# A feed-forward layer with its gradients: Square and Gelu ahead of evictions, a gate product ahead of a cubic, and two tails over 128 rows

## The chip, the core and the metric

The kernel runs on one core of a Trainium2 chip. The core has TensorE (PE, matmuls from SBUF into the eight PSUM banks), VectorE (DVE), ScalarE (ACT), GpSimd (POOL) and SyncE (SP), each with its own in-order queue of instructions; they wait for each other through semaphores. Transfers are issued from the queues of SP, ACT and POOL. The metric is the device time of one execution in microseconds (us), as the median over several runs.

## What is computed

```python
def _fwd_reference(x, w1, b1, w2, b2):        # x (1, 2048, 448), w1 (448, 1792), w2 (1792, 448)
    h = jnp.einsum("bsd,df->bsf", x, w1) + b1
    h = _gelu(h)                              # tanh approximation
    return jnp.einsum("bsf,fd->bsd", h, w2) + b2

def reference(x, w1, b1, w2, b2, grad_out):
    out, vjp = jax.vjp(_fwd_reference, x, w1, b1, w2, b2)
    return (out, *vjp(grad_out))              # out, and gradients of x, w1, b1, w2, b2
```

Everything that comes in and goes out is bfloat16. With u = x w1 + b1 and q = grad_out w2^T, the kernel needs h = gelu(u), gh = gelu'(u) q, out = h w2 + b2, the gradient of x, gh w1^T, and the products over the 2048 rows for the gradients of the weights.

## The kernel before

The 2048 rows are cut into 4 blocks of 512 columns of the transposed data, and the 1792 hidden features into 14 tiles of 128, taken two at a time. A *pair* is one block with two such tiles; there are 28, numbered f or k from 0, seven to a block. For a pair, TensorE computes u into two PSUM banks ("pu") and q into two ("pq"). 448 = 3 x 128 + 64, so each product over the 448 has three full steps (`w1_f`, `w2T`) and a *tail* of 64 rows (`wt1` and the last slice of `xT`). The tails, like most other matmuls, run as 64-row halves of the array, one half beside the other (`half_product`, L259). The pairs 0, 1 and 2 at the start have their full steps over 128 rows (`pe_u_fulls`, L238), and the tails of 0 and 1 run alone, each as two 64-row matmuls (`pe_tails`, which calls `u_tail`).

Around a pair's products stands its elementwise work. ACT copies u with its bias to SBUF (`copy_u`, L339), computes Square (`act_square`, L348), Gelu (`act_gelu`, L345, which gives h), and later the tanh (`act_tanh`, L357). DVE computes the *cubic* from the Square (L376), *cubic\*u* (L378, what the tanh needs), *slope* and *slope\*h* (L380, L382), *both* (L385), *gate* (L387) and *gh*, the gate product, which reads q from PSUM and writes gh (L393). The list of names that `dve_chain` is given is the order of DVE's queue.

The pairs 0 to 11 are worked in *single steps*, i = 1 to 11 in a loop (and pair 0 ahead of it). In step i TensorE does u of pair f = i + 2 and q of pair i. From pair 12 on come *double steps*, n = 0 to 7, with pairs k = 12 + 2n and k + 1 together: `act_tanh`, `dve_gate` (L361 to L368 on both pairs), then gh of k + 1 and of k (`dve_gh`, L393), while TensorE does u of the next two pairs (`pe_u_rows`, in the first double step alone), tails, q (`pe_q_rows`), and u of the pairs after those. Step i = 11 and n = 0 are the *passage*.

A *unit* is 128 rows of out (kind "o", from h) or of the gradient of x (kind "x", from gh), over 28 half-row matmul slots for each of two row halves. When a unit is finished it stands in the list `finished`, and `evictions()` empties its bank: kind "x" on ACT (L431), kind "o" on DVE with the bias (L433), both into one of five staging tiles, from which POOL issues the transfer to the output (L434). In steps 7 to 11 TensorE fills its gaps with four units of kind "x", two in PSUM banks 2 and 3 (`later`) and two in one tile of two banks (`ahead`). Their matmuls stand in the list `slots`, ten slots to a step: 8 of ahead, 14 of later, 7 of ahead, 14 of later, 7 of ahead. The two of `later` finish at slot 43 and the two of `ahead` at slot 50, both in step 11.

The banks turn over. Pair 14's u goes into banks 0 and 1, which `copy_u(13)` frees, pair 15's into banks 2 and 3, which the evictions of `later` free. The q of pair 13 goes into bank pair 1, which the evictions of `ahead` free, and q of pair 12 into bank pair 0, which gh of pair 11 frees. The next units go into bank pair 1 after gh of pair 13.

The weights arrive in pieces by transfers whose order is written out by hand; SP issues most. At i = 6 `other_halves` loads the upper 64 rows of `wt1`, which serve the later blocks; until then only its lower 64 rows (`DL` = 64) hold anything. Block 0's transposed x is loaded 512 wide (`wide`), so its last slice has 64 rows of the tail and 64 rows that belong to the next row of x.

Of the kernel before, what the change touches and what calls it, by code (L numbers as in the profile page):

```python
# [19 lines left out]
def kernel(  # L20
# [15 lines left out]
    nc = tc.nc  # L36
    P = 128
    B, S, D = x.shape
    F = w1.shape[1]
    assert (B, S, D, F) == (1, 2048, 448, 1792)  # L40
    NS = S // P
    NF = F // P
    KF = D // P
    DL = D - KF * P
# [3 lines left out]
    NPAIR = NF // 2  # L48
    NSTEP = NB * NPAIR
    NSINGLE = 12  # L50
# [30 lines left out]
    wt1 = const.tile([P, F], BF16, name="wt1")  # L81
# [12 lines left out]
    xT, gT = {}, {}  # L94
# [44 lines left out]
    AZ = tmp.tile([P, 12, SB], BF16, name="AZ", tag="AZ", bufs=1)  # L139
    zero = AZ[:, 0, :]  # L140
    nc.vector.memset(zero, 0.0)
    nc.gpsimd.memset(b1_rows[:], 0.0)
    nc.gpsimd.dma_start(out=b1_rows[0:NF, :], in_=b1.rearrange("(ft p) -> ft p", p=P))
    xT[0] = blk.tile([P, KF + 1, SB], BF16, name="xT", tag="xT")
# [45 lines left out]
    PU, PQ = {}, {}  # L190
# [4 lines left out]
    def cols(p, a):  # L195
        return slice((2 * FP[p] + a) * P, (2 * FP[p] + a + 1) * P)

    def part_u(ks):
        return U4[:, 2 * (ks[0] % 2):2 * (ks[-1] % 2) + 2, :]
# [4 lines left out]
    def part_a(ks):  # L204
        k = ks[0]
        return place(4 * (k % 3) if k < NSINGLE else SETS[k // 2 % 2] + 2 * (k % 2), ks)

    def part_z(ks):
        k = ks[0]
        return place(4 * (k % 3) + 2 if k < NSINGLE else 4 + 2 * (k % 2), ks)  # L210
# [14 lines left out]
    def open_u(f):  # L225
        b, p = divmod(f, NPAIR)
        if p == 0:
            hT[b] = blk.tile([P, NF, SB], BF16, name="hT", tag="hT")
        banks = (2, 3) if f == 1 else (0, 1) if f < NSINGLE + LEAD else order_a[2 * (f % 2):2 * (f % 2) + 2]
        PU[f] = [one_bank(n, "pu") for n in banks]  # L230

    def pe_u_fulls(f):
        b, p = divmod(f, NPAIR)
        open_u(f)
        for rs in halves if f == 0 else [slice(0, SB)]:
            for a in range(2):
                for kt in range(KF):
                    nc.tensor.matmul(PU[f][a][:, rs], lhsT=w1_f[:, kt, cols(p, a)], rhs=xT[b][:, kt, rs],  # L238
                                     start=(kt == 0 and rs.start == 0), stop=False, skip_group_check=True)
# [4 lines left out]
    def open_q(k):  # L244
        b, p = divmod(k, NPAIR)
        if p == 0:
            ghT[b] = blk.tile([P, NF, SB], BF16, name="ghT", tag="ghT")
        PQ[k] = two_banks(0 if k < NSINGLE else order_b[k % 2], "pq")
# [14 lines left out]
    def u_tail(f, a):  # L263
        b, p = divmod(f, NPAIR)
        hf = half(b not in WIDE)
        half_product(("u", f, a), PU[f][a][:], wt1[hf, cols(p, a)], xT[b][hf, KF, :], hf, False, True)

    def q_tail(k, a, swap=False):
        b, p = divmod(k, NPAIR)
        hf = half((b in WIDE) != swap)  # L270
        g = g_swap[b] if swap else gT[b][:, 0, :]
        half_product(("q", k, a), PQ[k][:, a, :], w2T[hf, 0, cols(p, a)], g[hf, :], hf, True, False)
# [5 lines left out]
    def pe_tails(fs, ks):  # L278
        cross = bool(fs) and bool(ks) and (fs[0] // NPAIR in WIDE) != (ks[0] // NPAIR in WIDE)
        for k in ks:  # L280
            open_q(k)
        us = [(f, a) for f in fs for a in range(2)]
        qs = [(k, a) for k in ks for a in range(2)]
        if not us and len(ks) == 2:
            for a in range(2):
                q_tail(ks[0], a)
                q_tail(ks[1], a, swap=True)
            return
        for n in range(max(len(us), len(qs))):
            if n < len(us):  # L290
                u_tail(*us[n])
            if n < len(qs):
                q_tail(*qs[n], swap=cross)
# [76 lines left out]
    def dve_chain(*names):  # L370
        for name in names:
            op, k = name.split()
            k = int(k)
            a_, z_ = part_a([k]), part_z([k])
            if op == "cubic":
                nc.vector.tensor_scalar(out=z_, in0=a_, scalar1=3.0 * GELU_C, scalar2=None, op0=ALU.add)  # L376
            elif op == "cubic*u":
                nc.vector.tensor_tensor(out=z_, in0=z_, in1=part_u([k]), op=ALU.mult)  # L378
            elif op == "slope":
                nc.vector.tensor_scalar(out=a_, in0=a_, scalar1=GELU_C, scalar2=-2.0, op0=ALU.add, op1=ALU.mult)  # L380
            elif op == "slope*h":
                nc.vector.tensor_tensor(out=a_, in0=a_, in1=rows(hT, [k]), op=ALU.mult)  # L382
            elif op == "both":
                both = place(4 * (k % 3), [k, k])
                nc.vector.tensor_scalar(out=both, in0=both, scalar1=1.0, scalar2=math.sqrt(0.5), op0=ALU.add, op1=ALU.mult)  # L385
            elif op == "gate":
                nc.vector.tensor_tensor(out=z_, in0=z_, in1=a_, op=ALU.mult)  # L387
            else:
                dve_gh(k)
# [20 lines left out]
    class Unit:  # L410
# [13 lines left out]
            self.done += 1  # L424
            self.slots += 4

        def evict(self):
            st = stg.tile([P, SB], BF16, name="st", tag="st")
            r = ROW0[self.b] + self.j * P
            if self.kind == "x":  # L430
                nc.scalar.copy(out=st[:, 0:D], in_=self.ps)  # L431
            else:
                nc.vector.tensor_tensor(out=st[:, 0:D], in0=self.ps, in1=b2_bc[:], op=ALU.add)  # L433
            nc.gpsimd.dma_start(out=(out2 if self.kind == "o" else gx2)[r:r + P, :], in_=st[:, 0:D])  # L434
# [27 lines left out]
                open_units.remove(un)  # L462
                finished.append(un)

    def evictions(most=NS):
        for un in finished[:most]:
            un.evict()
        del finished[:most]

    turns = {6: [(0, 0, 2)], 7: [(0, 2, 4)], 8: [(0, 4, 7)], 9: [(1, 0, 3)], 10: [(1, 3, 5)], 11: [(1, 5, 7)], 12: [(2, 0, 2)],  # L470
# [10 lines left out]
    def traffic(i):  # L481
# [5 lines left out]
        if i == 6:  # L487
            other_halves()

    pe_u_fulls(0)  # L490
    pe_tails([0], [])
    copy_u(0, "av")
    act_square([0])
    act_gelu([0])
    dve_chain("cubic 0", "cubic*u 0")
    pe_u_fulls(1)
    pe_tails([1], [])
    copy_u(1, "av")
    act_tanh([0])
    act_square([1])  # L500
# [23 lines left out]
    def tiles(p):  # L524
        return range(2 * p, 2 * p + 2)
# [13 lines left out]
    for i in range(1, NSINGLE):  # L539
        f = i + LEAD  # L540
        if i < 6:
            between = [(uns[1], False, tiles(i)), (uns[0], True, tiles(i)[:1]), (uns[0], True, tiles(i)[1:]), (uns[1], True, tiles(i))]
        elif i == 6:
            between = [(uns[0], True, tiles(i)), (uns[1], False, tiles(i)[:1]), (uns[1], False, tiles(i)[1:]), (uns[1], True, tiles(i))]
        else:
            if i == 7:
                ahead, later = xs, two_units((2, 3))
                slots = [(ahead, False, t) for t in range(6, NF)] + [(later, False, t) for t in range(NF)]
                slots += [(ahead, True, t) for t in range(NPAIR)] + [(later, True, t) for t in range(NF)]
                slots += [(ahead, True, t) for t in range(NPAIR, NF)]  # L550
            between = [slots[2 * c:2 * c + 2] for c in range(5)]
            del slots[0:10]
        open_u(f)
        open_q(i)
        side_by_side(u_of(f, 0, True), u_of(f, 1, True))
        fill(between[0])
        side_by_side(u_of(f, 1), u_of(f, 0))
        fill(between[1])
        pe_tail_pair(f, i, 1)
        pe_tail_pair(f, i, 0)  # L560
        fill(between[2])
        side_by_side(q_of(i, 0), q_of(i, 1))
        fill(between[3])
        side_by_side(q_of(i, 1, True), q_of(i, 0, True))
        if i < 6:
            units_side(uns[0], False, tiles(i + 1))
        elif i > 6:
            fill(between[4])
        if i > 1:
            act_tanh([i])  # L570
        if i == 6:
            evictions(2)
        copy_u(f, "aa")
        if i > 6:
            evictions()
        act_square([f])
        act_gelu([f])
        if i == 1:
            dve_chain("both 1", "cubic 2", "gate 1", "cubic*u 2", "slope 2", "gh 1", "slope*h 2", "cubic 3")
        elif i < NSINGLE - 1:  # L580
            dve_chain(f"both {i}", f"cubic*u {i + 1}", f"gate {i}", f"slope {i + 1}", f"gh {i}", f"slope*h {i + 1}", f"cubic {f}")
        else:
            dve_chain(f"both {i}", f"cubic*u {i + 1}", f"gate {i}", f"cubic {f}", f"gh {i}", f"cubic*u {f}")
        if i == 6:
            evictions()
            open_two(1, 2)
            xs = open_units[-2:]
            units_side(xs, False, range(0, 6))
        if i == 9:
            nc.gpsimd.dma_start(out=g_low[0:DL, :], in_=gT[1][DL:P, 0, :])  # L590
            g_swap[1] = g_low
        if i < 8 or i % 2:
            traffic(i if i < 8 else (i + 7) // 2)
        if i >= 6:
            stores(1 if i > 7 and i % 2 else 2, f - 1)
# [20 lines left out]
    for n in range(nq):  # L616
        i = 10 + n
# [206 lines left out]
```

## Time and profile before

| | |
|---|---|
| median of 3 runs | 270.81 us (270.75 to 271.07) |
| the profiled execution | 270.53 us |
| its span in the profile | 268.8 us |
| TensorE busy | 261.8 us, 97% of the span |
| VectorE busy | 175.0 us, 65% |
| ScalarE busy | 137.3 us, 51% |
| GpSimd busy | 42.0 us, 16% |
| granted TensorE clock | 0.998 of full speed |

The profile is one execution of the program. Its span runs from the first to the last instruction that it shows, and the execution's own time is 1.73 us longer. A row of a timeline gives the start and the length in us, engine, line of the program, operation, output and input tiles with their shapes, how many such instructions are merged (x2), and in brackets how long the engine stood idle ahead of it and what it waited for. Lengths of successive instructions of one engine overlap a little, since the next one starts in the pipeline before the last has left it; the ends of matmuls are modelled. A busy TensorE is therefore not TensorE at its peak.

### The profile page before, as it was taken

To read this page: it belongs to the slowest core of one execution; us is meant where nothing else is said; L and a number is where in the kernel's file an instruction comes from. 1 tells how busy PE (TensorE), PEld (TensorE's weight loads), DVE (VectorE), ACT (ScalarE), POOL (GpSimd) and SP (SyncE) were. 2 spreads that over 40 slices of the span, in tenths; PEclk is the share of its full clock that TensorE was granted. 3 is DMA by queue.
4 is the path that set the end of the run, shared out by engine and by line. 5 is a ranking of instruction groups with operands and counts; after the bars stand their busy time and mean duration, and the time that the engine had idled before them with its cause. 6 is when DMAs were issued, how large, how long until landed. Compare 5 with 4: busy or idle time off the path is not lost.

```text
span 268.8 us, 5196 instructions
## 1 busy us (share of the span) xinstructions
PE 261.8 (97%) x2170; PEld 164.7 (61%) x2170; DVE 175.0 (65%) x214; ACT 137.3 (51%) x163; POOL 42.0 (16%) x52
## 2 busy tenths in 40 slices
PE   7999999999979999999999999999999999999995
PEld 3356668888636665555657888874444665555554
DVE  1699999998698879687898831219999991000000
ACT  2899998878786867968668410022111111121111
POOL 1002004200302020110202030311600008900000
PEclk9999999999999999999999999999999999999999
DMA  7999999999999956172561449999511102999841
GB/s 176 235 269 198 154 233 193 268 243 217 221 224 232 235 166 156 37 191 50 152 152 41 80 91 272 353 191 238 143 39 39 49 22 48 215 220 214 206 123 34
DMA packets 111735, 44.47 MB, mean 165 GB/s; under 512 B 91040, under 2 KB 110576, under 8 KB 111712
## 3 DMA queue, kind: packets, MB, share of 16 engines
q1 hardware_dynamic: 104608, 36.14, 63.3%
q0 software_dynamic: 1856, 4.30, 5.9%
q10 hardware_dynamic: 5248, 3.71, 4.7%
q8 instruction: 17, 0.28, 0.4%
q14 instruction: 6, 0.05, 0.1%
HBM read 7.23 MB, written 14.23 MB: 80 GB/s over the span
## 4 chain that ended last, share of the span: by engine, by line
PE 94%; DMA 2%; ACT 1%; DVE 1%; issue 1%
PE ps L259 31%; PE ps_v L776 16%; PE pq L259 15%; PE pu L259 14%; PE ps_w L744 14%; PE ps_w L755 2%; DMA xT<-in_x_dram 2%; PE pu L238 2%; DVE ghT L393 1%; ACT U L339 0%; ACT st L431 0%; ACT AZ L348 0%; PE ps L421 0%; DVE AZ L378 0%; ACT st L779 0%
## 5 line engine op out<-in xcount | busy, mean ns | idle before, releaser
L259 PE MATMUL pq<-gT,w2T 64*128 64x512 bf16 x386 | 58.0, 376 | 0.0
L259 PE MATMUL ps<-w_sb,hT 64*128 64x448 bf16 x440 | 52.6, 349 | 1.1 <-DVE ghT L393 1.1
L259 PE MATMUL ps<-w1T_sb,ghT 64*128 64x448 bf16 x448 | 51.2, 349 | 0.0
L259 PE MATMUL pu<-xT,w_f 64*128 64x512 bf16 x300 | 44.0, 376 | 0.8 <-ACT U L339 0.8
L339 ACT ACTIVATE U<-pu,b1T 128x512 bf16<-128x512 f32 x53 | 32.8, 684 | 19.4 <-PE pu L259 19.4
L776 PE MATMUL ps_v<-g_nat,h_nat 128*128 128x448 bf16 (+1 forms) x240 | 42.6, 340 | 0.0
L393 DVE SCALAR_TENSOR_TENSOR ghT<-AZ,pq 128x1024 bf16<-128x1024 bf16 x28 | 33.9, 1219 | 13.3 <-PE pq L259 12.6
L434 POOL DMA_DIRECT2D out_dram<-st x32 | 19.7, 618 | 137.8 <-DVE st L433 75.6
L259 PEld LDWEIGHTS <-ghT 64*128 64x128 bf16 x448 | 33.9, 94 | 10.3
L259 PEld LDWEIGHTS <-hT 64*128 64x128 bf16 x440 | 29.4, 94 | 16.0 <-issue 1.5
L259 PEld LDWEIGHTS <-w2T 64*128 64x128 bf16 x392 | 29.8, 94 | 11.8 <-DMA w2T<-in_w_dram 0.3
L744 PE MATMUL ps_w<-gh_nat,x_nat 128*128 128x512 bf16 (+1 forms) x192 | 36.5, 352 | 0.0
L776 PEld LDWEIGHTS <-h_nat 128*128 128x128 bf16 x240 | 23.3, 98 | 19.3 <-DMA out_dram<-st 0.3
L357 ACT ACTIVATE AZ<-AZ 128x1024 bf16<-128x1024 bf16 (+1 forms) x20 | 27.8, 1390 | 9.0 <-DVE AZ L353 7.3
L730 DVE TENSOR_TENSOR acc<-acc,gh_nat 128x1792 f32<-128x1792 f32 x14 | 30.0, 2142 | 0.5
L744 PEld LDWEIGHTS <-x_nat 128*128 128x128 bf16 x192 | 18.7, 98 | 17.9 <-issue 0.4
L348 ACT ACTIVATE AZ<-U 128x1024 bf16<-128x1024 bf16 (+1 forms) x21 | 28.2, 1341 | 0.9 <-DVE U L341 0.4
L345 ACT ACTIVATE hT<-U 128x1024 bf16<-128x1024 bf16 (+1 forms) x22 | 27.9, 1274 | 0.0
L259 PEld LDWEIGHTS <-w_f 64*128 64x128 bf16 x300 | 21.0, 94 | 11.2 <-issue 1.4
L779 ACT CAST st<-ps_v 128x448 bf16<-128x448 f32 (+1 forms) x15 | 7.6, 507 | 34.8 <-PE ps_v L776 34.8
L431 ACT CAST st<-ps 128x448 bf16<-128x448 f32 x16 | 7.8, 536 | 29.6 <-PE ps L259 28.0
L747 ACT CAST st<-ps_w 128x512 bf16<-128x512 f32 (+1 forms) x12 | 6.4, 532 | 27.8 <-PE ps_w L744 27.8
(52 smaller groups left out, 190.0 us busy)
## 6 DMA issues: line engine op xcount, KB each, us to landing
hT_dram<-hT SPq DMA_DIRECT2D x28, 256.0 KB, 3.5
out_dram<-st POOLq DMA_DIRECT2D x32, 112.0 KB, 4.6
x_nat<-in_x_dram SPq DMA_DIRECT2D x1, 1792.0 KB, 10.3
g_nat<-in_grad_out_dram SPq DMA_DIRECT2D x1, 1792.0 KB, 15.5
out_dram<-st ACTq DMA_DIRECT2D x13, 112.0 KB, 3.3
out_dram<-st ACTq DMA_DIRECT2D x9, 128.0 KB, 1.7
w_f<-in_w_dram SPq DMA_DIRECT2D x5, 192.0 KB, 3.9
w_sb<-in_w_dram SPq DMA_DIRECT2D x4, 224.0 KB, 3.8
```

The costliest lines, as they stand in the source:

```text
L259: mm = nc.tensor.matmul(ps, lhsT=w, rhs=m, start=start, stop=stop, tile_position=(hf.start, 0), skip_group_check=True)
L339: nc.scalar.activation(out=dst, in_=PU[f][a][:], func=ACT.Identity, bias=bias)
L345: nc.scalar.activation(out=rows(hT, r), in_=part_u(r), func=ACT.Gelu_apprx_tanh)
L348: nc.scalar.activation(out=part_a(ks), in_=part_u(ks), func=ACT.Square, scale=math.sqrt(3.0 * GELU_A * GELU_C))
L357: nc.scalar.activation(out=z, in_=z, func=ACT.Tanh, scale=-1.0 / 3.0)
L393: nc.vector.scalar_tensor_tensor(out=rows(ghT, [k]), in0=part_z([k]), scalar=1.0, in1=PQ[k][:], op0=ALU.subtract if single else ALU.add, o ...
L431: nc.scalar.copy(out=st[:, 0:D], in_=self.ps)
L434: nc.gpsimd.dma_start(out=(out2 if self.kind == "o" else gx2)[r:r + P, :], in_=st[:, 0:D])
L730: nc.vector.tensor_tensor(out=v, in0=in0, in1=gh_nat[:, b, :, j, :], op=ALU.add)
L744: nc.tensor.matmul(ps[:, 0:n * P], lhsT=x_nat[:, st_, kt * P:(kt + 1) * P], rhs=gh_nat[:, b, ft0:ft0 + n, j, :], start=(st_ == 0), stop=(s ...
L776: nc.tensor.matmul(ps[:, 0:w], lhsT=h_nat[ft][:, st_, :], rhs=g_nat[:, st_, h * w:(h + 1) * w], start=(st_ == 0), stop=(st_ == NS - 1))
L779: nc.scalar.copy(out=o[:, 0:w], in_=ps[:, 0:w])
```

## The change

Three things are changed.

- At the front, the upper 64 rows of `wt1` in columns 256 to 767 are set to zero by a memset on DVE, and the tails of pairs 0 and 1 run as matmuls over all 128 rows, whose upper half multiplies those zeros.
- In step 11 the evictions are split. ACT evicts the first finished unit ahead of Square 13 and Gelu 13; the second is evicted by DVE with a plain copy, behind gate 11; the last two are left to the call at the start of n = 0, behind Gelu 13. The calls of `evictions()` in steps 7 to 10, ahead of the Square, are gone.
- In the DVE order of step 11, gh 11 stands ahead of cubic 13 instead of behind it.

```diff
     nc.vector.memset(zero, 0.0)
+    nc.vector.memset(wt1[DL:P, 256:768], 0.0)
...
-        def evict(self):
+        def evict(self, by=None):
...
-            if self.kind == "x":
+            if self.kind == "x" and by is not None:
+                nc.vector.tensor_copy(out=st[:, 0:D], in_=self.ps)
+            elif self.kind == "x":
                 nc.scalar.copy(out=st[:, 0:D], in_=self.ps)
...
-    def evictions(most=NS):
+    def evictions(most=NS, by=None):
         for un in finished[:most]:
-            un.evict()
+            un.evict(by)
         del finished[:most]
...
+    def pe_tail_zeros(f):
+        b, p = divmod(f, NPAIR)
+        for a in range(2):
+            nc.tensor.matmul(PU[f][a][:], lhsT=wt1[:, cols(p, a)], rhs=xT[b][:, KF, :], start=False, stop=True, skip_group_check=True)
+
     pe_u_fulls(0)
-    pe_tails([0], [])
+    pe_tail_zeros(0)
...
     pe_u_fulls(1)
-    pe_tails([1], [])
+    pe_tail_zeros(1)
...
         copy_u(f, "aa")
-        if i > 6:
-            evictions()
+        if i == NSINGLE - 1:
+            evictions(1)
         act_square([f])
         act_gelu([f])
...
-            dve_chain(f"both {i}", f"cubic*u {i + 1}", f"gate {i}", f"cubic {f}", f"gh {i}", f"cubic*u {f}")
+            dve_chain(f"both {i}", f"cubic*u {i + 1}", f"gate {i}")
+            evictions(1, "v")
+            dve_chain(f"gh {i}", f"cubic {f}", f"cubic*u {f}")
```

## Prediction

> **What bounds the kernel now.** I read the trace from the outside in. First the busy time by stretch: start, microseconds, then busy time and instruction count of TensorE (PE), weight loads (PEld), VectorE (DVE), ScalarE (ACT) and GpSimd (POOL). The two stretches are the passage from single steps to double steps, and most of what follows it.
>
> ```profile
> 67.67:77.70 10.03, 7.79 (x64) 4.41 (x61) 7.79 (x10) 8.71 (x10) 1.64 (x4) 1.00 1.16 214
> 77.70:222.90 145.20, 145.20 (x1285) 91.02 (x1285) 110.16 (x107) 65.20 (x71) 20.24 (x28) 1.00 0.59 141
> ```
>
> After 77.70 TensorE is busy for all of the 145.20 us, so from there the end moves with the moment at which that stretch begins. In the 10.03 us before it, TensorE works 7.79 us. That is where time can be had, and the next three views, timelines of ACT, DVE and PE through the passage (start, length, instruction, and in brackets the idle time ahead and its releaser), say what the hole hangs on.
>
> ```profile
> 65.16 1.26 ACT L339 ACTIVATE U<-pu,b1T 128x512 bf16<-128x512 f32 x2 [0.67 <-PE pu L259]
> 66.31 0.96 ACT L431 CAST st<-ps 128x448 bf16<-128x448 f32 x2
> 67.68 0.97 ACT L431 CAST st<-ps 128x448 bf16<-128x448 f32 x2 [0.41 <-PE ps L259]
> 68.54 1.07 ACT L348 ACTIVATE AZ<-U 128x1024 bf16<-128x1024 bf16 x1
> 69.49 1.06 ACT L345 ACTIVATE hT<-U 128x1024 bf16<-128x1024 bf16 x1
> 71.83 1.91 ACT L357 ACTIVATE AZ<-AZ 128x2048 bf16<-128x2048 bf16 x1 [1.28 <-DVE AZ L378]
> 73.65 0.67 ACT L339 ACTIVATE U<-pu,b1T 128x512 bf16<-128x512 f32 x1
> ```
>
> ACT copies pair 13's two halves (65.16), evicts two units, waits 0.41 us for TensorE to finish two more units, evicts those (67.68), and only then does Square 13 (68.54) and Gelu 13 (69.49). Inputs of the Square were there at 66.42, where the copies end.
>
> ```profile
> 65.73 0.69 DVE L387 TENSOR_TENSOR AZ<-AZ 128x1024 bf16<-128x1024 bf16 x1
> 69.64 0.43 DVE L376 TENSOR_SCALAR AZ<-AZ 128x1024 bf16<-128x1024 bf16 x1 [3.22 <-ACT AZ L348]
> 69.98 1.21 DVE L393 SCALAR_TENSOR_TENSOR ghT<-AZ,pq 128x1024 bf16<-128x1024 bf16 x1
> 71.11 0.68 DVE L378 TENSOR_TENSOR AZ<-AZ,U 128x1024 bf16<-128x1024 bf16 x1
> 71.71 0.69 DVE L361 TENSOR_SCALAR AZ<-AZ 128x2048 bf16<-128x2048 bf16 x1
> 72.50 1.23 DVE L363 TENSOR_TENSOR AZ<-AZ,hT 128x2048 bf16<-128x2048 bf16 x1
> 73.77 0.69 DVE L364 TENSOR_SCALAR AZ<-AZ 128x2048 bf16<-128x2048 bf16 x1
> 74.37 0.69 DVE L367 TENSOR_SCALAR AZ<-AZ 128x2048 bf16<-128x2048 bf16 x1
> 75.10 1.22 DVE L368 TENSOR_TENSOR AZ<-AZ 128x2048 bf16<-128x2048 bf16 x1
> 76.42 2.35 DVE L393 SCALAR_TENSOR_TENSOR ghT<-AZ,pq 128x1024 bf16<-128x1024 bf16 x2
> ```
>
> DVE stands 3.22 us before "cubic 13" (L376), which needs that Square. Behind it in the same queue stands gate product 11, "gh 11" (L393 at 69.98), which does not need it. From 69.64 to the products 13 and 12 (76.42) DVE has no gap worth naming: it is one chain.
>
> ```profile
> 66.36 0.91 PE L259 MATMUL pq<-gT,w2T 64*128 64x512 bf16 x6
> 67.01 0.64 PE L259 MATMUL ps<-w1T_sb,ghT 64*128 64x448 bf16 x4
> 67.39 2.85 PE L259 MATMUL pu<-xT,w_f 64*128 64x512 bf16 x24
> ...
> 71.25 0.37 PE L259 MATMUL pq<-g_low,w2T 64*128 64x512 bf16 x1 [0.36 <-DVE ghT L393]
> ...
> 71.48 2.30 PE L259 MATMUL pq<-gT,w2T 64*128 64x512 bf16 x18
> 74.37 0.37 PE L259 MATMUL pu<-xT,w_f 64*128 64x512 bf16 x1 [0.59 <-ACT U L339]
> 74.94 0.80 PE L259 MATMUL pu<-xT,w_f 64*128 64x512 bf16 x5 [0.20 <-ACT U L339]
> ...
> 77.70 0.56 PE L259 MATMUL ps<-w_sb,hT 64*128 64x448 bf16 x4 [1.09 <-DVE ghT L393]
> ```
>
> TensorE waits in three places: for gh 11 to free bank pair 0 (71.25), for ACT's copies, which stand behind the tanh (74.37, 74.94), and for gh 13 to free bank pair 1 (77.70). The last ends last, so **the bound in the passage is DVE's chain from cubic 13 to gh 13**, held up by ACT's order.
>
> **Part by part, the passage.** TensorE's last product of pair 11 ends at 66.36 + 0.91 = 67.27; from then on gh 11 may run. The new order on ACT: copies to 66.42, one eviction from 66.31 (from the second pair's start to the Square behind it are 68.54 - 67.68 = 0.86, so 0.43 for each eviction), so Square 13 at 66.31 + 0.43 = 66.74, done at 66.74 + 1.07 = 67.81; Gelu at 66.74 + (69.49 - 68.54) = 67.69; the two evictions of the late units at 68.64 and 69.07, done by about 69.60.
>
> The new order on DVE: gate 11 from 65.73 to 66.42, then the moved eviction. DVE shows no such plain copy out of PSUM; the nearest row is its own eviction with a bias, of the same 128x448 f32 tile:
>
> ```profile
> 83.64 1.16 DVE L433 TENSOR_TENSOR st<-ps,b_bc 128x448 bf16<-128x448 f32 x2
> 84.71 0.68 DVE L367 TENSOR_SCALAR AZ<-AZ 128x2048 bf16<-128x2048 bf16 x1
> ```
>
> Two take 1.16, so 0.58 each. From below the cost is nothing; from above I take gh's 1.21, which also reads PSUM but over 1024 elements. I take 0.58: it ends by 66.42 + 0.58 = 67.00, ahead of 67.27, and costs nothing, because DVE would wait for TensorE anyway. At the upper end it ends at 67.63 and costs 0.36. The bank it empties is wanted by the second pair of TensorE's 24 matmuls that begin at 67.39, six of them later (one follows another after (2.85 - 0.37) / 23 = 0.108, so at 67.39 + 0.65 = 68.04): 1.0 us of room.
>
> So gh 11 starts at about 67.30 instead of 69.98. Behind it comes cubic 13, 71.11 - 69.98 = 1.13 later, at 68.43 (Square done at 67.81: 0.62 of room), then "cubic*u 13", 69.98 - 69.64 = 0.34 later, at 68.77, and the double step's gate (L361) 0.60 later at 69.37 instead of 71.71. **The chain comes 2.34 us forward**: 2.68 from gh 11, less 0.34 because the cubic now stands inside the chain instead of in front of it.
>
> What is late next? Gate L363 needs Gelu 13: done at 67.69 + 1.06 = 68.75, wanted at 70.16. L367 needs the tanh. That may start when cubic*u 13 ends (68.77 + 0.68 = 69.45) and ACT's evictions are issued, so at about 69.50, and ends at 71.41; DVE reaches L367 at 74.37 - 2.34 = 72.03: 0.62 of room. Gh 13 needs TensorE's products 13: TensorE no longer waits at 71.25, its eight tails follow the 24 matmuls at 69.98 and last 8 x 0.108, and it comes to the 18 at about 70.8 instead of 71.48, done by 72.8; gh 13 starts at 74.08. Copies 15 and 14 follow the tanh at 71.32, so TensorE's 74.37 becomes about 72.8. Then it waits, longer than now, for gh 13: units at 77.70 - 2.34 = 75.36. All three old waits shrink into one of about 1.2 us. The late units' banks are wanted by the tails at 69.98 and free at 69.60: 0.4 of room on TensorE, and 1.3 more before gh 13 notices.
>
> The eviction calls taken out of steps 7 to 10 emptied nothing, since by the slot list all four units finish in step 11, two of them at slot 43 of 50 and two at slot 50. They cost nothing. After 77.70 DVE, ACT and TensorE all come 2.34 earlier together, and TensorE is busy throughout, so I carry the whole 2.34 to the end.
>
> **Part by part, the front.** The tails of pairs 0 and 1 now take 128 rows. Timeline of TensorE around the tail of pair 1, a weight load, a DMA issue and the first memset:
>
> ```profile
> 8.19 0.59 PE L238 MATMUL pu<-xT,w_f 128*128 128x512 bf16 x2
> 8.72 0.60 PE L259 MATMUL pu<-xT,wt 64*128 64x512 bf16 x2
> 9.26 0.82 PE L238 MATMUL pu<-xT,w_f 128*128 128x512 bf16 x3
> ```
> ```profile
> 11.84 0.09 PEld L259 LDWEIGHTS <-w2T 64*128 64x128 bf16 x1 [0.34 <-DMA w2T<-in_w_dram]
> ```
> ```profile
> 8.34 1.30 SPq L134 DMA_TRANSPOSE w2T<-in_w_dram  x1
> ```
> ```profile
> 0.85 0.27 DVE L141 MEMSET AZ<- 128x256 uint32 x1 [0.85 <-PEq L808]
> ```
>
> Matmuls of one kind follow each other by (0.82 - 0.38) / 2 = 0.22, where 0.38 is one matmul's length (0.82 is that of three). From the last 128-row matmul (8.19 + 0.21 = 8.40) over the two tails to the next at 9.26 are 0.86; three steps of 0.22 would be 0.66. So each pair saves up to 0.20, both 0.40; at the least nothing. But at 11.84 TensorE waits for a weight transfer issued at 8.34, which has nothing to do with TensorE's pace. It has waited 0.34 there already; coming earlier it waits up to 0.74. **I take 0.** From 11.84 to the passage TensorE has no wait, so nothing earlier carries over. The extra memset is half the rows of the one shown, about 0.27 by that row, with nothing waiting on DVE until the bias arrives; it costs nothing, and even if the first tail weights had to wait for it, the 0.34 of the transfer is cover.
>
> **Sum.** The profiled execution took 270.53, of which 268.8 is span, 1.73 around it. Less 2.34: span 266.46, time 268.19. The median before is 270.81, 0.28 above the profiled run; on it the forecast is 268.47, say 268.5.
>
> **Rivals.** POOL's issues of the evictions' transfers, in order of time:
>
> ```profile
> 67.14 1.10 POOL L434 DMA_DIRECT2D out_dram<-st  x2 [18.37 <-ACT st L431]
> 68.51 1.07 POOL L434 DMA_DIRECT2D out_dram<-st  x2 [0.27 <-ACT st L431]
> 84.56 1.48 POOL L434 DMA_DIRECT2D out_dram<-st  x2 [14.98 <-DVE st L433]
> ```
>
> *POOL holds up DVE.* Now the four issues of the passage run while DVE is idle (66.42 to 69.64). After the change all four lie beside DVE's chain. If an issue stops DVE for as long as it lasts, two that meet it cost 2 x 0.54 = 1.1: 269.6. If all four do at the length they have beside a busy DVE, 1.48 / 2 = 0.74, that is 2.96 against 2.34, and the kernel is **slower**: 271.4. It decides from 2.34 / 4 = 0.585 an issue on. Against it: at 84.56 an issue starts ahead of L367 (84.71), and L367 takes 0.68, its usual 0.69 (74.37); the issues got longer, not DVE. The Trainium skill, page "SBUF — State Buffer", section "SBUF: two separate sides", has this rule: VectorE in a two-port mode and GpSimd share one port pair as an exclusive lock, whichever starts first keeps it, the other blocks fully. By that rule POOL, being first at 84.56, would have delayed L367; the trace shows only the other half, a software-issued DMA stretched beside VectorE. The rule's price would be that of this rival.
>
> *The front pays too.* If the transfer awaited at 11.84 is not what held TensorE, up to 0.40 more: 268.1.
>
> *The Square does not come forward*: if the unit evicted first were one of the late ones, ACT would still wait until 67.68, Square would come at 68.11 and only one eviction (0.43) be won: 270.4. The slot list speaks against it.
>
> **Chances.** Forecast 0.72 (its own range 268.2 to 268.8); front pays 0.07; POOL's issues or the dear eviction eat up to 1.1: 0.10; Square stays 0.04; slower by POOL 0.07. About 0.2% (0.54 us) is what a measurement of this kernel can tell from no change. Faster 0.89, same 0.04, slower 0.07. The range 267.9 to 269.6 takes in the first three cases, with the front's 0.40 and the dear eviction's 0.36 inside it.
>
> **What would show it.** On ACT, one eviction, Square 13 near 66.7, Gelu, two evictions, tanh near 69.5. On DVE, the eviction ending by 67.0, gh 11 at 67.3 and no 3.22 wait; L361 near 69.4; gh 13 near 74.1. On TensorE, no wait at the tails, one of about 1.2 for gh 13, units near 75.4, and the weight load at 11.84 still there with a longer wait. I am wrong if gh 11 starts later than 67.6, if L367 or gh 13 waits for ACT or TensorE, or if a wait appears after the units begin.

## The result and the profile after

The changed kernel took **268.80 us** (median of 12 runs, 268.19 to 277.72) against 270.81 before: a ratio of 0.9924, with a 95% interval of 0.9907 to 0.9940. It was run twice more, with the first and with the last group of the experiments below: 268.83 (ratio 0.9895, 0.9867 to 0.9923) and 268.89 (0.9919, 0.9900 to 0.9938), called the second and the third time. The forecast was 268.5. Medians count every execution and ratios leave out those over 1.5% above the fastest of their kernel, here 273.20 us and the first profiled one (277.72, at a granted TensorE clock of 0.95 of full), without which the median is 268.61. The rows here are from another profiled execution, of the third time, with a granted clock of 1.00 and a span of 266.6 us. Of gh 11 first alone, whose profile has a granted clock of 0.91 between 40 and 60 us, only what comes from the passage on is compared. Lines of the program stand one or three lower than before (L394 is the old L393, L362 the old L361, L434 the old L431, L436 the old L433); L432 is the new eviction on DVE.

First ACT through the passage (start, length, instruction, idle time ahead and its releaser):

```profile
65.32 1.26 ACT L340 ACTIVATE U<-pu,b1T 128x512 bf16<-128x512 f32 x2 [0.67 <-PE pu L260]
66.47 0.53 ACT L434 CAST st<-ps 128x448 bf16<-128x448 f32 x1
66.88 1.08 ACT L349 ACTIVATE AZ<-U 128x1024 bf16<-128x1024 bf16 x1
67.84 1.06 ACT L346 ACTIVATE hT<-U 128x1024 bf16<-128x1024 bf16 x1
68.79 0.97 ACT L434 CAST st<-ps 128x448 bf16<-128x448 f32 x2
69.69 1.91 ACT L358 ACTIVATE AZ<-AZ 128x2048 bf16<-128x2048 bf16 x1
```

One eviction, Square, Gelu, two evictions, tanh, with no wait between them. Then DVE:

```profile
65.89 0.68 DVE L388 TENSOR_TENSOR AZ<-AZ 128x1024 bf16<-128x1024 bf16 x1
66.50 0.62 DVE L432 CAST st<-ps 128x448 bf16<-128x448 f32 x1
67.38 1.22 DVE L394 SCALAR_TENSOR_TENSOR ghT<-AZ,pq 128x1024 bf16<-128x1024 bf16 x1 [0.27 <-PE pq L260]
68.52 0.42 DVE L377 TENSOR_SCALAR AZ<-AZ 128x1024 bf16<-128x1024 bf16 x1
68.97 0.69 DVE L379 TENSOR_TENSOR AZ<-AZ,U 128x1024 bf16<-128x1024 bf16 x1
69.58 0.69 DVE L362 TENSOR_SCALAR AZ<-AZ 128x2048 bf16<-128x2048 bf16 x1
...
74.29 2.35 DVE L394 SCALAR_TENSOR_TENSOR ghT<-AZ,pq 128x1024 bf16<-128x1024 bf16 x2
```

The 3.22 us hole is gone. The eviction takes 0.62, and DVE still waits 0.27 for TensorE behind it; gh 11 starts at 67.38, and gh 13 at 74.29 (76.42 before). Last TensorE, from the 24 matmuls of u to the units:

```profile
67.55 2.75 PE L260 MATMUL pu<-xT,w_f 64*128 64x512 bf16 x24
...
71.00 2.11 PE L260 MATMUL pq<-gT,w2T 64*128 64x512 bf16 x18
72.95 0.81 PE L260 MATMUL pu<-xT,w_f 64*128 64x512 bf16 x6
73.59 0.81 PE L260 MATMUL pq<-gT,w2T 64*128 64x512 bf16 x6
74.24 0.38 PE L260 MATMUL pu<-xT,w_f 64*128 64x512 bf16 x2
75.56 1.69 PE L260 MATMUL ps<-w_sb,hT 64*128 64x448 bf16 x16 [0.94 <-DVE ghT L394]
```

Of the three waits one is left, 0.94 for gh 13.

Executions of one kernel differ by half a microsecond and more ahead of these 24 matmuls: in the two profiles of the change they start at 68.10 and 67.55. Some profiles show where: TensorE waits for the first transfers, and near 47 us for the gradient of block 1 (0.80 in Square first, 1.64 in gh 0 first, 1.65 in the gate split, nothing in both profiles of the change). So I cut each profile at two points: the start of those 24 matmuls, and the start of the units. The stretch between them, the **passage**, is what the change is about; behind it comes the **rest**, up to the end of the span, which the traces hold to a hundredth.

| kernel | 24 matmuls start | units start | passage | rest | median and ratio (95%) |
|---|---|---|---|---|---|
| before | 67.39 | 77.70 | 10.31 | 191.06 | 270.81 |
| the change, second time | 68.10 | 76.21 | 8.11 | 191.06 | 268.83, 0.9895 (0.9867 to 0.9923) |
| the change, third time | 67.55 | 75.56 | 8.01 | 191.05 | 268.89, 0.9919 (0.9900 to 0.9938) |
| tails alone | 67.89 | 78.20 | 10.31 | 191.04 | 271.03, 0.9999 (0.9975 to 1.0023) |
| passage alone | 67.41 | 75.47 | 8.06 | 191.05 | 268.39, 0.9906 (0.9869 to 0.9942) |
| gh 11 first alone | 72.92 | 82.28 | 9.36 | 191.04 | 269.96, 0.9961 (0.9934 to 0.9987) |
| Square first, cubic ahead of gh 11 | 68.78 | 77.28 | 8.50 | 191.05 | 269.66, 0.9947 (0.9923 to 0.9972) |
| both evictions on ACT | 67.77 | 75.88 | 8.11 | 191.06 | 268.68, 0.9917 (0.9904 to 0.9930) |
| w2 load from ACT | 68.55 | 76.70 | 8.15 | 191.05 | 269.85, 0.9960 (0.9933 to 0.9987) |
| gate split | 69.97 | 77.78 | 7.81 | 192.07 | 270.02, 0.9960 (0.9943 to 0.9977) |
| gh 0 first | 69.44 | 77.59 | 8.15 | 191.05 | 269.17, 0.9942 (0.9921 to 0.9962) |
| early slope | 67.49 | 74.56 | 7.07 | 192.03 | 268.90, 0.9920 (0.9898 to 0.9943) |
| early slope and gh 0 | 67.83 | 74.90 | 7.07 | 191.98 | 268.72, 0.9919 (0.9899 to 0.9939) |

The passage is shorter by 2.2 to 2.3 us in both profiles of the change, and the rest is what it was. The experiments were run in three groups: the second time of the change to gh 11 first alone, Square first to the gate split, and the third time with the last three rows. Their medians of the kernel before were 271.27, 271.31 and 270.70. What the ratios give for the change, 2.1, 2.8 and 2.2 us, holds the scatter ahead of the passage in both kernels; the passages do not.

### The profile page after: what moved, and what is told of

It is laid out like the page before. It is cut to its first block, busy times and chain, and to the rows that moved or that the text cites. A ratio compares the mean times of both kernels' runs of the same rounds, so it can differ in the third digit from the quotient of the medians.

```text
span 276.0 us, 5199 instructions
## 1 busy us (share of the span) xinstructions
PE 270.1 (98%) x2170; PEld 161.9 (59%) x2170; DVE 176.3 (64%) x216; ACT 136.6 (50%) x162; POOL 41.5 (15%) x52
## 4 chain that ended last, share of the span: by engine, by line
PE 91%; DVE 3%; SPq 3%; DMA 1%; issue 0%; ACT 0%; DVEq 0%
PE ps L260 32%; PE ps_v L786 16%; PE pq L260 14%; PE pu L260 14%; PE ps_w L754 14%; PE ps_w L765 2%; SPq L113 1%; DMA w2T<-in_w_dram 1%; DVE ghT L394 1%; SPq L147 0%; SPq L150 0%; DVE AZ L364 0%; DVE AZ L369 0%; DVE AZ L365 0%; DVE AZ L379 0%
## 5 line engine op out<-in xcount | busy, mean ns | idle before, releaser
L260 PE MATMUL ps<-w_sb,hT 64*128 64x448 bf16 x440 | 50.8, 360 | 0.6 <-DVE ghT L394 0.6
L394 DVE SCALAR_TENSOR_TENSOR ghT<-AZ,pq 128x1024 bf16<-128x1024 bf16 x28 | 33.9, 1220 | 16.9 <-PE pq L260 16.2
L786 PE MATMUL ps_v<-g_nat,h_nat 128*128 128x448 bf16 (+1 forms) x240 | 44.2, 350 | 0.0
L260 PE MATMUL pu<-xT,w_f 64*128 64x512 bf16 x300 | 43.1, 388 | 0.0
L260 PEld LDWEIGHTS <-ghT 64*128 64x128 bf16 x448 | 32.2, 97 | 13.8
L260 PEld LDWEIGHTS <-hT 64*128 64x128 bf16 x440 | 30.4, 97 | 15.6 <-issue 0.9
L754 PE MATMUL ps_w<-gh_nat,x_nat 128*128 128x512 bf16 (+1 forms) x192 | 37.9, 363 | 0.0
L260 PEld LDWEIGHTS <-w2T 64*128 64x128 bf16 x392 | 27.6, 96 | 15.8 <-DMA w2T<-in_w_dram 0.7
L260 PEld LDWEIGHTS <-w_f 64*128 64x128 bf16 x300 | 19.4, 96 | 12.4
L434 ACT CAST st<-ps 128x448 bf16<-128x448 f32 x15 | 7.3, 537 | 29.5 <-PE ps L260 29.5
```

The source lines that it names most:

```text
L260: mm = nc.tensor.matmul(ps, lhsT=w, rhs=m, start=start, stop=stop, tile_position=(hf.start, 0), skip_group_check=True)
L394: nc.vector.scalar_tensor_tensor(out=rows(ghT, [k]), in0=part_z([k]), scalar=1.0, in1=PQ[k][:], op0=ALU.subtract if single else ALU.add, o ...
L754: nc.tensor.matmul(ps[:, 0:n * P], lhsT=x_nat[:, st_, kt * P:(kt + 1) * P], rhs=gh_nat[:, b, ft0:ft0 + n, j, :], start=(st_ == 0), stop=(s ...
L786: nc.tensor.matmul(ps[:, 0:w], lhsT=h_nat[ft][:, st_, :], rhs=g_nat[:, st_, h * w:(h + 1) * w], start=(st_ == 0), stop=(st_ == NS - 1))
```

## The experiments

The theory was that DVE's chain from gh 11 to gh 13 sets the passage, and that TensorE's front is held by a weight transfer, so that the 128-row tails gain nothing. The rivals were POOL's issues, the front paying, and the Square or the product alone being what counts.

**The change again**, and once more with the last group:

> The change as it is, for a profile at the full granted clock. Theory (DVE's chain from gh 11 to gh 13 sets the end of the passage): about 2.0 to 2.4 us less than before, gh 11 near 67.3, no 3.22 us wait ahead of cubic 13, the gate L362 (formerly L361) near 69.4, units near 75.4, and one wait of about 1.2 us for gh 13. Rival (POOL's issues hold up DVE): L362 to L369 longer than their 0.69 and 1.22, gh 13 later than 74.3.

> The change as it is, beside the three variants of this group. Passage (first of the 24 u matmuls to the units) 8.1 us as in its earlier profile, rest (units to the end) 191.0 us; the stretch ahead of it scatters by half a microsecond and more with the landing of the first transfers. 2.0 to 2.6 us less than before.

The order of events is as expected: the table and rows above are these. The second time everything stands later by 0.5 to 0.7 than the third, since the 24 matmuls start at 68.10; so its gh 13, at 74.93, is no sign of the rival. POOL's issues the second time, and DVE beside them:

```profile
67.85 1.10 POOL L437 DMA_DIRECT2D out_dram<-st  x2 [18.38 <-ACT st L434]
70.17 1.38 POOL L437 DMA_DIRECT2D out_dram<-st  x2 [1.22 <-ACT st L434]
```
```profile
70.22 0.69 DVE L362 TENSOR_SCALAR AZ<-AZ 128x2048 bf16<-128x2048 bf16 x1
```

POOL begins at 70.17, ahead of DVE's L362 (70.22); DVE keeps its 0.69, the operations behind it keep their 0.69 and 1.23 too, and the two issues grow from 1.10 to 1.38. The rival in which POOL holds DVE up falls.

**Tails alone** (only the memset and the two `pe_tail_zeros` of the change).

> The two 128-row tails alone. Theory (the w2T transfer that lands at about 11.84 holds TensorE): no change, 270.8 within 0.2 us; the units ahead of it start up to 0.4 earlier and the wait there grows by as much. Rival (the front pays): up to 0.40 less, with the first q matmul earlier than 11.8.

No change that the runs can tell: ratio 0.9999, 0.9975 to 1.0023. The interval does not exclude a few tenths either way; what the tails do is read from the traces below. The longer wait for the transfer did not show: the first q matmul is at 11.96 with no wait ahead of it, and the wait that the profile has is 0.23 at 17.32, for gh 0.

**Passage alone** (the change without these lines):

```diff
-    nc.vector.memset(wt1[DL:P, 256:768], 0.0)
-    pe_tail_zeros(0)
+    pe_tails([0], [])
-    pe_tail_zeros(1)
+    pe_tails([1], [])
```

> The passage alone, tails as before. Theory: all of the change's gain, 2.0 to 2.4 us less than before, within 0.2 us of the whole change. Rival (the front pays): up to 0.4 behind the whole change.

0.9906, with a passage of 8.06: all of the gain. The whole change in the same group has 0.9895, and the intervals cover each other.

**gh 11 first alone** (the kernel before, with one line changed):

```diff
-            dve_chain(..., f"gate {i}", f"cubic {f}", f"gh {i}", f"cubic*u {f}")
+            dve_chain(..., f"gate {i}", f"gh {i}", f"cubic {f}", f"cubic*u {f}")
```

> Only gh 11 ahead of cubic 13 in DVE's order; ACT's order and the evictions as before. Theory: gh 11 runs in the 3.22 us hole, cubic 13 still waits for the Square until 69.64, cubic*u 13 follows at 69.98 instead of 71.11, so 1.13 us less than before. Rival (the Square's place is all that counts): no gain, because cubic 13 starts no earlier.

Time ratio 0.9961, and a passage of 9.36, 0.95 shorter. DVE in this kernel:

```profile
72.89 1.22 DVE L393 SCALAR_TENSOR_TENSOR ghT<-AZ,pq 128x1024 bf16<-128x1024 bf16 x1 [0.94 <-PE pq L259]
75.22 0.43 DVE L376 TENSOR_SCALAR AZ<-AZ 128x1024 bf16<-128x1024 bf16 x1 [1.11 <-ACT AZ L348]
75.68 0.69 DVE L378 TENSOR_TENSOR AZ<-AZ,U 128x1024 bf16<-128x1024 bf16 x1
```

The product fills the hole, and DVE still waits 1.11 for the Square. Cubic\*u comes 0.46 behind the cubic, not 0.34 as I had taken; that is most of the 0.18 between 0.95 and the 1.13 expected.

**Square first, the old order on DVE** (the passage alone, with `cubic 13` ahead of `gh 11`):

```diff
-            dve_chain(f"gh {i}", f"cubic {f}", f"cubic*u {f}")
+            dve_chain(f"cubic {f}", f"gh {i}", f"cubic*u {f}")
```

> ACT's order and the eviction on DVE as in the change, but cubic 13 ahead of gh 11 as before; tails as before. Theory: cubic 13 at 67.84 behind the Square (67.81), gh 11 at 68.18, cubic*u 13 at 69.31, so 1.80 us less than before: 0.54 behind the whole passage. Rival (gh 11's place counts for nothing once the Square is early): the same as the passage alone, 2.0 to 2.4.

The passage is 8.50, 1.81 shorter, and 0.44 longer than with both edits. The two edits overlap: alone they are worth 0.95 and 1.81, together 2.25. The time ratio, 0.9947 against 0.9917 for both evictions on ACT in the same group, is 0.8 us; the passages (8.50 and 8.11) explain 0.4 of it, and TensorE's wait of 0.80 for the gradient, at 46.40, stands ahead of the passage.

**Both early evictions on ACT** (the passage alone):

```diff
-            evictions(1)
+            evictions(2)
-            evictions(1, "v")
```

> As the passage alone, but both units that finish first are evicted by ACT ahead of the Square, none by DVE. Theory: Square 0.43 later, done at 68.24, still ahead of the 68.43 at which DVE would take cubic 13; tanh at the same 69.5; the same gain as the passage alone within 0.2 us. Rival (the eviction on DVE is part of the gain): 0.4 us less gain.

A passage of 8.11, against 8.06. DVE then waits 0.89 ahead of gh 11 instead of 0.31, for TensorE: the eviction on DVE costs nothing and brings nothing.

**The w2 load from ACT's queue** (the change):

```diff
     load_rest(nc.scalar, 512, 1024)
+    load_w2(nc.scalar, 2, 4)
-    load_w2(nc.sync, 2, 4)
```

> The whole change, and the load of rows 2 to 3 of w2 issued from ACT's queue instead of SP's, so that SP issues the block gradient and the awaited w2T transfer 0.52 earlier (4.08 instead of 4.60, 7.82 instead of 8.34). Theory (that transfer holds the front): the first q matmul 0.4 to 0.5 us earlier, and as much off the whole change's time. Rival (something else holds it): nothing gained.

Neither came about: it was slower. Its ratio is 0.9960 (0.9933 to 0.9987), against 0.9895 to 0.9924 for the change in other groups, and 0.9917 (0.9904 to 0.9930) for both evictions on ACT in the same one. TensorE at the front, and the issue of the weight transfer w2T, which SP did begin earlier, at 7.91:

```profile
6.02 1.51 PE L239 MATMUL pu<-xT,w_f 128*128 128x256 bf16 x12 [0.94 <-DMA xT<-in_x_dram]
```
```profile
12.85 0.39 PE L260 MATMUL pq<-gT,w2T 64*128 64x512 bf16 x1 [0.37 <-DMA w2T<-in_w_dram]
```
```profile
7.91 2.56 SPq L134 DMA_TRANSPOSE w2T<-in_w_dram  x1
```

The first x came 0.6 later (6.02, against 5.38 before), and the awaited w2T 1.0 later than before and 0.7 later than in the change (12.85, against 11.84, 12.16 and 12.13), although its issue began 0.43 earlier than before. That issue took 2.56 instead of the 1.30 of before and so ended later (10.47 against 9.64). TensorE does wait for that transfer, but its landing is not set by its place in the queue alone. Why the issue grew, and what the best order would be, stays open; this is one profiled execution.

**Gate split** (the change; in the first double step the gate is done in halves, both slopes first, then 13's second half and gh 13, then 12's):

```diff
-        dve_gate(ks, evictions)
+        if n == 0:
+            for q in ks[::-1]:
+                gate_slope(q)
+            gate_tanh(ks[1])
+        else:
+            dve_gate(ks, evictions)
...
-        for q in ks[::-1]:
-            dve_gh(q)
+        dve_gh(ks[1])
+        if n == 0:
+            gate_tanh(ks[0])
+        dve_gh(ks[0])
```

> The whole change, and the gate of the first double step done pair by pair (13 first, gh 13 ahead of the second half of gate 12), so that gh 13 starts about 1.1 us earlier. Theory (the units wait for gh 13 about 1.2 us): 0.9 to 1.2 us less than the whole change. Rival (another wait ends as late, ACT's copies or TensorE's own products): nothing, or less than 0.4.

It lost. The passage got shorter by only 0.2 to 0.3, since the slope of 12 still stood ahead of gh 13 and five operations became ten (72.14 to 78.09 in its trace). And the rest got longer by 1.0: TensorE had a new wait 8 us after the units began.

```profile
85.95 0.37 PE L260 MATMUL pq<-gT,w2T 64*128 64x512 bf16 x1 [0.76 <-DVE st L436]
```

By its ratio, 0.9960 against 0.9917 for both evictions on ACT in the same group, it is 1.2 us slower; the passage and the rest explain 0.7 of it. The profiled execution was late ahead of the passage as well, where at 47.59 it waited 1.65 for the gradient of block 1.

**Early slope** (the change; ACT evicts both early units, DVE does the first two operations of gate 12 ahead of gh 11, and the tanh and the gate of 13 come ahead of those of 12):

```diff
-            evictions(1)
+            evictions(2)
...
-            evictions(1, "v")
+            gate_slope(i + 1)
             dve_chain(f"gh {i}", f"cubic {f}", f"cubic*u {f}")
...
-        act_tanh(ks)
-        dve_gate(ks, evictions)
+        if n == 0:
+            act_tanh(ks[1:])
+            act_tanh(ks[:1])
+            gate_slope(ks[1])
+            nc.vector.tensor_scalar(out=part_a(ks), in0=part_a(ks), scalar1=-0.5, scalar2=None, op0=ALU.add)
+            gate_tanh(ks[1])
+        else:
+            act_tanh(ks)
+            dve_gate(ks, evictions)
```

The products are issued as in the split kernel.

> The change, with both early units evicted by ACT, the first two operations of gate 12 done by DVE ahead of gh 11, and the rest of the first double step's gate and its tanh done for pair 13 first. Theory (after the change DVE's chain to gh 13 is still the bound of the passage, by the 0.94 that TensorE waits): gh 13 ends about 1.1 us earlier, the wait of 0.94 gone or under 0.2, the passage 7.0 to 7.3 us instead of 8.1, 0.8 to 1.1 us less than the change, and gh 12 no later than now, so that the rest stays at 191.0. Rival (smaller operations cost DVE what they win, as when the whole gate was split): passage no shorter than 7.8, or the rest longer than 191.3.

The passage did get 0.94 to 1.04 shorter, and the wait ahead of the units is gone: they follow TensorE's own work at 74.56. So the theory was right on the passage, and wrong on the rest, which got 1.0 longer: the ratio, 0.9920, is that of the change (0.9919). DVE and TensorE 6 to 8 us into the rest:

```profile
80.87 0.69 DVE L365 TENSOR_SCALAR AZ<-AZ 128x2048 bf16<-128x2048 bf16 x1
81.47 1.15 DVE L436 TENSOR_TENSOR st<-ps,b_bc 128x448 bf16<-128x448 f32 x2
```
```profile
80.30 0.35 PE L260 MATMUL ps<-w_sb,hT 64*128 64x448 bf16 x1
...
82.68 0.37 PE L260 MATMUL pq<-gT,w2T 64*128 64x512 bf16 x1 [0.52 <-DVE st L436]
```

These units stand in bank pair 1, which the next q wants; DVE evicts them (L436) only when it has worked off all that stands ahead. In the change the same eviction begins at 81.50, no later:

```profile
81.50 1.16 DVE L436 TENSOR_TENSOR st<-ps,b_bc 128x448 bf16<-128x448 f32 x2
```
```profile
82.71 0.37 PE L260 MATMUL pq<-gT,w2T 64*128 64x512 bf16 x1
```

There it ends at 82.66 and TensorE takes the bank at 82.71. So this order brings the units forward by 1.0 and their eviction not at all. DVE was not busy throughout, though. In the early slope it stands 0.53 ahead of gh 13, for TensorE's products:

```profile
73.23 1.22 DVE L394 SCALAR_TENSOR_TENSOR ghT<-AZ,pq 128x1024 bf16<-128x1024 bf16 x1 [0.53 <-PE pq L260]
```

And the last matmul of these units ends at 80.30 + 0.35 = 80.65, ahead of L365 (80.87), which DVE still does before the eviction. So the 0.94 that TensorE waits after the change is real, and this order gives it back. Whether another wins it stays open: the eviction ahead of L365, or on ACT, was not tried.

**gh 0 first**, on the change and on the early slope:

```diff
-    dve_chain("cubic*u 1", "gate 0", "slope 1", "gh 0", "slope*h 1")
+    dve_chain("cubic*u 1", "gate 0", "gh 0", "slope 1", "slope*h 1")
```

> The change, with gh 0 ahead of slope 1 in DVE's order at the start. Theory (the front is set by pair 0's elementwise chain, whose gh 0 frees the bank of q 1 at about 16.8): gh 0 ends about 0.33 earlier after the first copies, TensorE's first q tail of pair 1 comes 0.15 to 0.4 earlier measured from those copies, the passage and the rest as in the change; 0.15 to 0.4 us less in all. Rival (the w2T transfer alone sets the front, as the prediction had it): the q tail of pair 1 at the same distance from the first q of pair 0, nothing gained.

> Both of the last two edits together. Theory: the gains add, 0.95 to 1.5 us less than the change. Rival: as in either alone.

Neither is faster than its base (ratios 0.9942 against 0.9919, and 0.9919 against 0.9920), so both theories missed. What they show of the front comes in the next part.

## Why the prediction was right, point by point

- **The chain on DVE.** Right. Gh 11 was put at 67.30 and is at 67.38 in a profile whose matmuls run 0.16 later; Square at 66.74 (66.88), tanh at 69.50 (69.69), L361 at 69.37 (69.58), gh 13 at 74.08 (74.29). Both edits are needed: 0.95 and 1.81 alone.
- **Its size.** 2.34 was forecast, 2.20 to 2.30 came. The term that was too large is the step from cubic to cubic\*u: put at 0.34, the spacing between the cubic and a gh that does not read its result; it measures 0.45 where the next operation reads it (68.52 to 68.97). That is 0.11 of the chain.
- **The new eviction on DVE.** Put at 0.58, it takes 0.62 and is hidden, since DVE still waits 0.27 for TensorE.
- **What is late next.** Right in the passage: one wait left, forecast at about 1.2, measured as 0.94.
- **The rest carries everything.** Right: 191.05 to 191.06 in before and in both profiles of the change, because DVE came forward with TensorE, as the prediction had it. In the change the eviction ends at 82.66 and TensorE takes bank pair 1 at 82.71; before they were at 84.80 and 84.85, with the same 0.05 between them. The early slope shows that DVE has to come along: there the units came 1.0 earlier, the eviction did not, and the 1.0 was given back. The prediction named no such limit.
- **The front.** The amount taken, 0, is not contradicted; the saving itself came as worked out. TensorE in the change, second time, around the tail of pair 1:

```profile
7.94 1.46 PE L239 MATMUL pu<-xT,w_f 128*128 128x512 bf16 x6
9.24 0.59 PE L496 MATMUL pu<-xT,wt 128*128 128x512 bf16 x2
9.67 1.46 PE L239 MATMUL pu<-xT,w_f 128*128 128x512 bf16 x6
```

From 7.94 to 9.67 are 1.73 for eight matmuls, 0.216 each; before it were 1.94 (7.32 to 9.26), 0.21 more, against the 0.20 worked out. The Trainium skill, page "TensorEngine Tiling (Array Packing)", section "Tiling Modes", says that changing the tiling mode drains TensorE; the 0.1 at each of the two changes agrees with it.

The reason given was incomplete, though. The wait at the transfer did not grow towards 0.74. The second time and in the tails alone the profile has none there; the third time it is 0.37, at 12.13, behind an issue at 8.62 instead of 8.34, and 0.31 was lost earlier, to the weights of pair 1's full steps:

```profile
7.49 1.47 PE L239 MATMUL pu<-xT,w_f 128*128 128x512 bf16 x6 [0.31 <-DMA w_f<-in_w_dram]
...
12.13 0.39 PE L260 MATMUL pq<-gT,w2T 64*128 64x512 bf16 x1 [0.37 <-DMA w2T<-in_w_dram]
```

And "From 11.84 to the passage TensorE has no wait" was wrong: there is a second gate, at the first q tail of pair 1. Before:

```profile
7.21 0.69 ACT L339 ACTIVATE U<-pu,b1T 128x512 bf16<-128x512 f32 x1 [3.91 <-PE pu L259]
```
```profile
15.55 1.21 DVE L393 SCALAR_TENSOR_TENSOR ghT<-AZ,pq 128x1024 bf16<-128x1024 bf16 x1
```
```profile
16.59 0.38 PE L259 MATMUL pu<-xT,wt 64*128 64x512 bf16 x1
16.82 0.37 PE L259 MATMUL pq<-gT,w2T 64*128 64x512 bf16 x1
```

Gh 0 ends at 15.55 + 1.21 = 16.76, and the tail that needs its bank starts at 16.82, 0.23 behind the one beside it. From the first copy (7.21) to the end of gh 0 are 9.55. In the change, second time, where the first matmuls came late, the copy is at 7.93, and the view of TensorE's tails shows the wait openly:

```profile
17.54 0.37 PE L260 MATMUL pq<-gT,w2T 64*128 64x512 bf16 x1 [0.25 <-DVE ghT L394]
```

7.93 + 9.55 = 17.48. The third time the copy came at 7.00, gh 0 ended at 16.55, and the tail at 16.88 follows the transfer instead, 4.75 behind the first q matmul. In gh 0 first on the change it does so too (12.13 and 16.89), which is the rival's sign. So the front ends at the later of two: the w2T transfer, which the tails do not touch, and pair 0's elementwise chain, which they bring forward by the switch saved ahead of the first copies, 0.1. Gh 0 first shortens that chain, but only from 9.55 to 9.43 (7.38 to 16.81 in the early slope with gh 0): gh 0, which reads the gate's result, starts 0.80 behind the gate, where slope 1 started 0.60 behind it, and that takes back 0.20 of the 0.33 expected. A tenth here is below what these runs can tell.

- **The range.** It held 268.80. The difference to the forecast is 0.3 (0.1 for the 268.61). The chain is 0.1 of it; the remainder lies inside the scatter of the front, whose end was anywhere from 67.41 to 68.10 in the three profiles of the change and of the passage alone.

## What to carry to other kernels

Where an engine's in-order queue holds an instruction that waits, look at what stands behind it and does not need the wait; here a gate product waited 2.7 us behind a Square's consumer, and the Square stood behind evictions that nobody needed yet. Moving work forward is worth what the next in-order queue can follow: after the change, taking away the last visible wait of 0.94 gave nothing in the order that was tried, because DVE came to an eviction 7 us later no earlier than it had. To compare variants whose executions scatter at the start, cut each trace at two events of the stream that sets the end, and compare the pieces.

## What the runs showed of the hardware

- On DVE, behind a cubic of 0.42 to 0.43 over 128x1024, cubic\*u, which reads it, starts after 0.45 to 0.46, and a gh that does not read it after 0.34. Behind gate 0 the operation that reads it starts after 0.80, another after 0.60. So in these rows an independent operation between two dependent ones is worth 0.11 to 0.20.
- A POOL transfer issue that starts 0.05 ahead of a DVE operation on SBUF does not slow that operation (0.69), while the pair of issues takes 1.38, against 1.10 for the pair before it.
- With one 224 KB load issued from ACT's queue instead of SP's, the issue of an awaited transfer on SP began 0.43 earlier than before but took 2.56 instead of 1.30; TensorE had its data 1.0 later, and the first x 0.6 later, in the one profiled execution.
